# Moving the load, cast and DMA transposition of two batches' states to a later place in a fused attention and maxout kernel

## The chip, the cores and the metric

One core of one Trainium2 chip. The metric is device time in microseconds (us) of one execution. A profile covers the span from the first to the last instruction, some 1.8 us shorter than the time that is measured. Engines in the profile: PE is TensorE (PEld its weight loads), ACT is ScalarE, DVE is VectorE, POOL is GpSimd, SP is SyncE, which here only issues DMAs. L200 is line 200 of the kernel file.

## The reference

`x` is (8, 8, 512, 64): batch, head, token, width. `state` is (8, 8, 32, 64). Attention goes both ways between tokens and states; the result, 4352 rows of 512, goes through a maxout layer of three weights W and an output weight. The kernel folds the states into W (tile `G`), which changes nothing here.

```python
scores = x @ state.T / 8;    a  = softmax(scores);   xread = a @ state
scores2 = state @ x.T / 8;   a2 = softmax(scores2);  sread = a2 @ x
x = concatenate([xread, sread], axis=2)          # -> (8*544, 512)
h = maximum(maximum(x @ w1, x @ w2), x @ w3)
out = h @ w_out                                  # float32
```

## The kernel before

The order of instructions on each engine is set by hand and is the order of the calls below. States are kept for two batches at a time in a block-diagonal tile `bds[k]`; `bds[1]` serves batches 2 and 3. It is made in four steps: load in float32, cast (each state twice side by side), transposition, and placing (two copies into the diagonal blocks).

```python
def load_st(k, eng):
    eng.dma_start(out=st_f[k], in_=state[2 * k:2 * k + 2]...)          # 128 KB, float32
def states_cast(k, cast):
    cast(out=st[k], in_=st_f[k].unsqueeze(2).to_broadcast((128, 4, 2, D)))
def states_transpose(k, dma):
    if dma:
        nc.sync.dma_start_transpose(out=stT[k], in_=st[k]...)
    else:                                                              # TensorE, used for k = 0
        for t in range(4):
            nc.tensor.transpose(stT[k][:, t, :], st[k][:, t]..., ident)
def states_place(k, copy):
    for c in range(2):
        copy(out=bds[k][r, :, :, c, :]..., in_=stT[k][r]...)
def states(k, copy):
    states_transpose(k, False); states_place(k, copy)
def x_pad(b): nc.gpsimd.tensor_copy(...)     # x of a batch into columns with ones between
```

The schedule around it, with cuts (`pool` is a copy on GpSimd, `act` on ScalarE, `dve` on VectorE):

```python
    x_transpose(1, 0, act)
    load_st(1, nc.scalar)
    ...
    softmax(1, 1, 2, (nc.gpsimd.tensor_mul, J))
    load_w(3, (2,))                          # the last part of W
    states_cast(1, pool)
    states_transpose(1, True)
    load_x(2)
    nc.gpsimd.dma_start(out=wout_sb, in_=moe_w_out...)
    for k in range(2, B // 2):
        load_st(k, nc.gpsimd)
    load_x(3)
    load_x(4)
    ...                                      # GpSimd clears x_pads and bds[1..3]
    states_place(1, pool)
    x_maxout(0, 1)
    ...
    x_maxout(1, 2)
    for k in range(2, B // 2):
        states_cast(k, pool)
    x_pad(2)
    x_maxout(0, 4)
    x_transpose(2, 0, dve)
    x_maxout(0, 5)
    g_cols(1, (4, 5), defer=(False, True))
    x_transpose(2, 1, act)
    x_maxout(1, 3)
    scores(2, 0, 2)                          # first reader of bds[1]
    softmax(2, 0, 2, (nc.gpsimd.tensor_mul, J))
    x_transpose_dma(3)
    states_transpose(2, True)
```

The softmax here doesn't subtract the row's maximum and nothing guards it: scores larger than these inputs give would overflow.

## Time and profile before

| | before |
|---|---|
| time, median of 4 runs (lowest to highest) | 154.53 us (154.02 to 155.31) |
| span of the profiled run | 152.9 us |
| TensorE busy | 145.8 us, 95% |
| `bds[1]` complete | 31.0 us |
| scores of batch 2 start on TensorE | 33.55 us |
| from there to the end | 119.3 us |

A timeline line reads: start, length, engine, line of the kernel, operation, output from input, shapes, how many; in brackets how long the engine stood idle before it and what ended that. In the chain of work that ended last, the name after the two times is what the whole program waited for at that moment. The lines of before are in the prediction. The chain view puts the start of an instruction where its predecessor's modelled end is, so it has 33.72 us for the scores where the timeline has 33.55; from here on starts are the timeline's.

### The profile page before, as it was taken

The page shows a single profiled execution, that of the slowest core. Times are in us where ns is not written, and L with a number is a line of the kernel's source. Part 1 is how long each engine was busy: PE and PEld are TensorE (multiplying, and loading weights), DVE is VectorE, ACT ScalarE, POOL GpSimd, SP SyncE. Part 2 cuts the span into 40 slices and gives each one's busy share as a digit, 9 for nine tenths or more (in the row PEclk, how much of TensorE's full clock was granted, in tenths as well). Part 3 has the DMA queues.
Part 4 walks back from the last instruction along what each step waited for, and adds up shares of the span by engine and source line. Part 5 has one row for each costly group of instructions (what it writes and reads, how often), then busy time and mean ns, then how long its engine had stood idle before and what let it go on. Part 6 is the DMA issues. An engine that isn't in the chain of part 4 may idle for free.

```text
span 152.9 us, 3490 instructions
## 1 busy us (share of the span) xinstructions
PE 145.8 (95%) x1382; PEld 70.7 (46%) x1382; DVE 97.8 (64%) x177; ACT 94.0 (62%) x145; POOL 66.4 (43%) x80
## 2 busy tenths in 40 slices
PE   6987899999999999999999999999999999999990
PEld 2544443554453445344534453445344556665450
DVE  3488768768827685768576767776767684566010
ACT  3655788686848656865686568656865637332440
POOL 8988599737421882088308310821082100100410
PEclk9999999999999999999999999999999999999999
DMA  3999999999939999989485973061206120210473
GB/s 119 189 181 203 194 166 85 202 237 197 268 63 178 143 187 281 177 115 199 172 178 81 190 166 138 7 198 46 107 14 196 47 103 0 83 57 0 162 254 137
DMA packets 37520, 21.85 MB, mean 143 GB/s; under 512 B 22528, under 2 KB 35072, under 8 KB 37504
## 3 DMA queue, kind: packets, MB, share of 16 engines
q0 software_dynamic: 17184, 14.94, 54.3%
q1 hardware_dynamic: 20032, 6.43, 22.8%
q10 hardware_dynamic: 288, 0.26, 0.6%
q8 instruction: 11, 0.18, 0.5%
q14 instruction: 5, 0.04, 0.1%
HBM read 15.20 MB, written 8.91 MB: 158 GB/s over the span
## 4 chain that ended last, share of the span: by engine, by line
PE 83%; POOL 5%; DMA 5%; ACT 2%; issue 1%; DVE 1%; POOLq 0%; DVEq 0%
PE pw L377 43%; PE po L416 28%; DMA w<-in_moe_w_dram 5%; PE pg L301 4%; POOL w L109 2%; PE ps L200 2%; POOL x L80 2%; PE pg L327 1%; PE psr L267 1%; ACT G L333 1%; PE ph L408 1%; ACT t L382 1%; POOL a L220 1%; DVE t L385 0%; DVE den L213 0%
## 5 line engine op out<-in xcount | busy, mean ns | idle before, releaser
L377 PE MATMUL pw<-aT,G 128*128 128x512 bf16 x288 | 69.2, 379 | 0.4 <-ACT G L333 0.4
L385 DVE TENSOR_TENSOR t<-t,pw 128x512 bf16<-128x512 bf16 (+1 forms) x54 | 35.0, 649 | 29.0 <-ACT t L382 28.5
L416 PE MATMUL po<-wout,ht 128*128 128x512 bf16 x198 | 47.2, 379 | 0.2 <-DVE t L385 0.2
L377 PEld LDWEIGHTS <-G 128*128 128x128 bf16 x288 | 26.7, 98 | 32.1 <-issue 2.9
L386 DVE TENSOR_TENSOR ht<-t,pw 128x512 bf16<-128x512 bf16 (+1 forms) x54 | 35.5, 657 | 5.6
L382 ACT CAST t<-pw 128x512 bf16<-128x512 f32 (+1 forms) x54 | 30.5, 565 | 12.0 <-PE pw L377 11.2
L419 ACT COPY osb<-po 128x512 f32<-128x512 f32 x33 | 19.3, 586 | 28.5 <-PE po L416 28.5
L416 PEld LDWEIGHTS <-ht 128*128 128x128 bf16 x198 | 18.8, 98 | 24.1 <-issue 2.8
L430 POOL DMA_DIRECT2D out_dram<-osb x14 | 7.9, 566 | 47.8 <-ACT osb L419 42.0
L220 POOL TENSOR_TENSOR a<-e,rden 128x1024 bf16<-128x1024 bf16 (+2 forms) x10 | 15.3, 1532 | 25.8 <-DVE rden L215 16.2
L308 ACT CAST G<-pg 128x1024 bf16<-128x1024 f32 x24 | 24.5, 1021 | 2.3 <-PE pg L301 1.6
L246 POOL COPY xp<-x 128x2048 bf16<-128x2048 bf16 x6 | 11.3, 1884 | 0.0
L213 DVE TENSOR_REDUCE den<-e 128x32 f32<-128x1024 bf16 (+1 forms) x10 | 10.0, 996 | 1.7 <-ACT e L205 1.6
L333 ACT CAST G<-pg 128x768 bf16<-128x768 f32 x11 | 8.8, 808 | 2.2 <-PE pg L327 2.2
L109 POOL DMA_DIRECT2D w<-in_moe_w_dram x12 | 9.2, 782 | 0.6 <-DMA x<-in_x_dram 0.6
L377 PE MATMUL pw<-ats,w 128*128 128x256 bf16 x72 | 8.7, 272 | 0.0
L205 ACT ACTIVATE e<-ps 128x1024 bf16<-128x1024 f32 x6 | 6.2, 1029 | 3.7 <-PE ps L200 3.7
L377 PEld LDWEIGHTS <-w 128*128 128x128 bf16 x72 | 7.0, 98 | 1.9
L301 PE MATMUL pg<-w,bd 64*32 64x512 bf16 x192 | 7.5, 381 | 0.0
L127 PE MATMUL idle<-zero 128*128 128x512 bf16 x16 | 6.1, 528 | 1.2 <-DVE zero L85 1.2
L153 POOL COPY bd<-stT 64x512 bf16<-64x512 bf16 x6 | 6.5, 1077 | 1.1 <-DMA stT<-st 0.9
L200 PEld LDWEIGHTS <-xT 128*128 128x128 bf16 x128 | 5.0, 98 | 2.1 <-DVE t L385 0.3
(61 smaller groups left out, 85.9 us busy)
## 6 DMA issues: line engine op xcount, KB each, us to landing
out_dram<-osb POOLq DMA_DIRECT2D x14, 512.0 KB, 3.6
x<-in_x_dram POOLq DMA_DIRECT2D x6, 512.0 KB, 9.2
w<-in_moe_w_dram POOLq DMA_DIRECT2D x6, 256.0 KB, 6.6
x<-in_x_dram POOLq DMA_DIRECT2D x3, 256.0 KB, 6.5
w<-in_moe_w_dram POOLq DMA_DIRECT2D x6, 128.0 KB, 6.7
wout<-in_moe_w_out_dram POOLq DMA_DIRECT2D x1, 768.0 KB, 11.6
out_dram<-osb SPq DMA_DIRECT2D x3, 256.0 KB, 2.0
x0f<-in_x_dram SPq DMA_DIRECT2D x1, 512.0 KB
```

Source lines behind the costliest of these rows:

```text
L109: nc.gpsimd.dma_start(out=w_slices(w_sb, c)[:, :, i, :], in_=w[:, :, m0 * 128:m1 * 128])
L220: mul(out=a[b][:, r, g0:g1].rearrange("p j g s n -> p j (g s) n"), in0=e[b][:, r, g0:g1].rearrange("p j g s n -> p j (g s) n"), in1=rden[: ...
L246: nc.gpsimd.tensor_copy(out=x_pads[b % 2][:, 2:2 + 2 * H * PW].rearrange("p (k c) -> p k c", c=PW)[:, :, 0:2 * D], in_=x_sb[b][:, 0:XW].re ...
L301: nc.tensor.matmul(ps[g][32 * s:32 * s + 32], bd(b, 2 * s + g)[64 * g:64 * g + 64, g, :], w_sb[64 * g:64 * g + 64, s, c0:c1], start=True, ...
L308: copy(out=G[b][:, :, c0:c1], in_=p[:, :, 0:n])
L333: copy(out=m_cols(G[b], m), in_=pv)
L377: nc.tensor.matmul(pw[i][:, 0:n], lhs(i, k), rhs(k), start=(k == 0), stop=(k == nk - 1))
L382: nc.scalar.copy(out=t0[:, 0:n], in_=pw[0][:, 0:n])
L385: nc.vector.tensor_max(t1[:, 0:n], t0[:, 0:n], pw[1][:, 0:n])
L386: nc.vector.tensor_max(ht[b][:, m, :], t1[:, 0:n], pw[2][:, 0:n])
L416: nc.tensor.matmul(p, ht[b][:, m, j * 128:(j + 1) * 128], wout_sb[:, m, :], start=(m == 0), stop=(m == NM - 1))
L419: act(out=o[:, j, :], in_=p)
```

## The change

The intent: the states of batches 2 and 3 are not needed before 33 us, so their load need not share the DMA engines with W, which is needed at 15 us. It is moved behind all of W; cast and transposition follow once it is in, and GpSimd fills the time of the transposition with the padding of x of batch 2.

```diff
     x_transpose(1, 0, act)
-    load_st(1, nc.scalar)
     sread(0)
...
     load_w(3, (2,))
-    states_cast(1, pool)
-    states_transpose(1, True)
+    load_st(1, nc.gpsimd)
     load_x(2)
...
     for k in range(1, B // 2):
         nc.gpsimd.memset(bds[k], 0.0)
-    states_place(1, pool)
+    states_cast(1, pool)
+    states_transpose(1, True)
     x_maxout(0, 1)
...
     x_maxout(1, 2)
+    x_pad(2)
+    states_place(1, pool)
     for k in range(2, B // 2):
         states_cast(k, pool)
-    x_pad(2)
     x_maxout(0, 4)
```

## The prediction

> **What bounds the kernel now.** I read the page first. The rows of busy shares put TensorE (PE) at 95% of a span of 152.9 us, and the row of slices (each digit a tenth of busy time, 3.8 us a slice) has nines from the seventh slice on. So from about 25 us to the end TensorE is the bound, and a gap put into that stretch is paid in full. The DMA row is at nine over the first eleven slices, up to some 40 us.
>
> ```profile
> PE 145.8 (95%) x1382; PEld 70.7 (46%) x1382; DVE 97.8 (64%) x177; ACT 94.0 (62%) x145; POOL 66.4 (43%) x80
> PE   6987899999999999999999999999999999999990
> DMA  3999999999939999989485973061206120210473
> ```
>
> Next the chain that ended last (start in us, length in us, what). It is TensorE from about 15 us on; before that it is a load of W, and then a short stretch over ScalarE, VectorE and GpSimd.
>
> ```profile
> 7.70 7.33 DMA w<-in_moe_w_dram
> ...
> 15.06 0.40 PE pg L327 x8
> ...
> 18.02 1.05 POOL a L220
> ...
> 32.42 1.29 PE pw L377 x6
> 33.72 0.47 PE ps L200 x16
> 34.18 1.29 PE po L416 x6
> ```
>
> The line to look at is L200 at 33.72: the scores of batch 2. They are the first readers of the block-diagonal states of batches 2 and 3 (tile bd, index 1), the only tile whose making the change moves. They follow the maxout before them without a gap. Third, the timeline of GpSimd (POOL), which makes that tile:
>
> ```profile
> 19.01 0.80 POOL L109 DMA_DIRECT2D w<-in_moe_w_dram  x1
> 19.82 0.62 POOL L136 CAST st<-stf 128x512 bf16<-128x512 f32 x1
> 20.37 0.89 POOL L70 DMA_DIRECT2D x<-in_x_dram  x1
> ...
> 25.05 2.82 POOL L479 MEMSET bd<- 128x1024 bf16 x3
> 28.80 2.20 POOL L153 COPY bd<-stT 64x512 bf16<-64x512 bf16 x2 [0.94 <-DMA stT<-st]
> 33.34 1.17 POOL L136 CAST st<-stf 128x512 bf16<-128x512 f32 x2 [2.33 <-DMA stf<-in_state_dram]
> 34.46 1.89 POOL L246 COPY xp<-x 128x2048 bf16<-128x2048 bf16 x1
> 37.38 1.91 POOL L220 TENSOR_TENSOR a<-e,rden 128x1024 bf16<-128x1024 bf16 x1 [1.04 <-DVE rden L215]
> ```
>
> The cast of the states is at 19.82, the transposition is issued right behind it, and it runs while GpSimd issues loads and clears tiles: of its whole latency GpSimd waits for only 0.94 us. The tile is complete at 31.0, which is 2.7 us before TensorE wants it. That 2.7 us is all the slack there is. Last, the DMA issues, asked for in small windows so that each line is one transfer (the last number is us from issue to landing): the states of batches 2 and 3 as loaded now, then their transposition at 20.46, then the same transposition of the next states at 39.81.
>
> ```profile
> stf<-in_state_dram ACTq DMA_DIRECT2D x1, 128.0 KB, 5.5
> stT<-st SPq DMA_TRANSPOSE x1, 8.2
> stT<-st SPq DMA_TRANSPOSE x1, 3.8
> ```
>
> The same shape took 8.2 us when the load of x of batch 2 and of w_out were in flight, and 3.8 us when the loads were over. This spread is the main uncertainty.
>
> **What the Trainium skill says.** (1) "DMA: Bandwidth & Descriptors", section "Queues, rings and completion order": each DMA engine goes round-robin between the queues that have work, packet by packet, so a transfer from one queue is slowed by traffic of the others. The trace agrees: 8.2 us against 3.8. (2) The same page, "Rules for kernel authors": to overlap a DMA with compute, issue it early and wait late. The kernel before does it (0.94 us waited of 8.2); the change does the reverse. (3) "TensorE: Matmul & The Clock Gate", "The HAM clock gate": TensorE falls to half its clock after an idle window of some 3.4 us. Here the only long idle stretch is the end: the last matmul ends at 149.2, and the windows view (busy us and count per engine, then granted clock, DMA share, GB/s) shows half clock 3.4 us later:
>
> ```profile
> 152.60:152.85 0.25, 0.00 (x0) 0.00 (x0) 0.00 (x0) 0.00 (x0) 0.00 (x0) 0.50 0.00 0
> ```
>
> So a stall of over about 3.4 us in mid-kernel may cost more than itself.
>
> **The change, part by part.** Work is neither added nor removed; instructions move. The order of instructions on each engine confirms it: TensorE and VectorE keep theirs, ScalarE loses one DMA issue, GpSimd gains one.
>
> *The load of the states, 128 KB, from ScalarE's queue at 9.6 us to GpSimd's queue behind the last part of W.* It lands at about 15.1 now, beside the part of W that the chain waits for until 15.02; TensorE stands 0.65 us for it. With that load away I choose that this part lands 0.3 us earlier (an estimate: 128 KB at the 203 GB/s of that stretch is 0.65 us, and about half of it lies ahead of that part's last bytes). Everything up to the scores of batch 2, GpSimd's stream too, moves up by 0.3 us. ScalarE's issue costs nothing; GpSimd pays about 0.57 us (two such issues take 1.14 in its timeline).
>
> *GpSimd's stream.* At 19.82 the cast of 0.62 goes and the issue of 0.57 comes, so the clearing of the tiles still ends at 25.05 + 2.82 = 27.87, or 27.6 with the 0.3. The load issued at 19.8 is behind only the last part of W (issued 19.01, landing 5.7 us later, at 24.7), so it has landed by about 26 and the cast doesn't wait. Cast 27.6 to 28.2; transposition issued at 28.2.
>
> *The transposition.* Its landing L is what decides. The padding of x of batch 2 (1.89 us) fills 28.2 to 30.1 of it; the rest GpSimd waits. At 28.2 the queue still holds the end of w_out, the other states and x of batches 3 and 4 (the last lands at 39.3 now), so it is the loaded case, not the quiet one. With the early transposition gone, those loads get ahead somewhat. I choose L = 6.8, between 5 and 8.5.
>
> *The placing.* 0.1 us after the landing two copies start, 2.20 us: the tile is complete at 28.2 + 6.8 + 0.1 + 2.2 = 37.3.
>
> *TensorE.* It would be ready for the scores at 33.7 - 0.3 = 33.4, and stands until 37.3: a stall of 3.9 us. Against now, the scores start 37.3 - 33.7 = 3.6 us later; in general L - 3.2. Behind them TensorE is back to back, so nearly all stays. Give-back: one idle of 0.17 us at 41.1 may go, -0.2. Clock: a stall of 3.9 us is a little over one idle window, so a quarter chance of a drop that costs about half of a window each time, some 2 us: +0.4 in the mean. The padding moved ahead of the placing, and the two later casts (1.17 us) behind it, cost nothing: the softmax product comes 3.7 us after the start of the scores anyway (37.38 against 33.72). Sum: 3.6 - 0.2 + 0.4 = +3.8, so 154.66 + 3.8 = 158.5 us.
>
> **The rivals.** *The transposition is quick.* With the early one gone the loads before it are done sooner, and the DMA queue thins. At L = 3.8 the scores start only 0.6 us late, and the time is about 155.2. For it: the second transposition took that. Against it: 1 MB of x is still to come at 28.2, and its last landing is at 39.3. *W lands much earlier and pays for it.* The chain's 0.65 us stand at 15.06 is the most that can be won there, so this can't outweigh the rest; and as GpSimd's stream is in the same chain, both move together. Were there no wait at the scores, the time would be 154.3. *The stall trips the clock.* With L = 8.2 the stall is over 5 us, half clock follows for some us, and the time is 154.66 + 5.0 + 2 = 161.7. *Another wait takes the place:* x of batch 2 lands at about 29.1 now, just ahead of its transposes at 29.3; one more load ahead of it could delay it, but the early transposition that shared the engines with it is gone, which should advance it instead. If it came later, that wait would be swallowed by the stall at the scores.
>
> **Range and chances.** L from 5 to 8.5 gives +1.8 to +5.3; with the give-back and the clock's part, 156.4 to 160.8, centre 158.5. The line of 2% is +3.1 us, that is L of about 6.2 with the other terms at their means; I put L above it a little more often than not. Faster by 2% would need 3 us out of a stretch where TensorE is idle for about that much in all: 0.01. Within 2%: 0.37. Slower: 0.62.
>
> **What would show it.** In the changed kernel's profile: the cast of these states on GpSimd at about 27.6, right behind the clearing, with no wait; a new wait of GpSimd's placing for the transposition, about 5 us instead of 0.94; a new wait of TensorE at L200 for the placing, 3 to 5 us, and scores at about 37 instead of 33.7; the chain going through GpSimd's clearing, the cast, the transposition and the placing; the wait for W at 15.06 shorter by a few tenths; the stretch from the scores to the end unchanged in length, or longer where the granted clock shows 0.50. The prediction is wrong if the transposition lands in 4 us or less, if the states' load lands late and the cast waits, or if the clock drops for a long time.

## The result, and the profile after

The changed kernel takes 161.06 us (median of 4 runs, 159.75 to 161.89), the kernel before 154.53. The ratio is 1.041, with a 95% interval from 1.032 to 1.05. A ratio here is the mean time of one kernel's fast runs over the mean of the other's fast runs of the same rounds, so it is not quite the ratio of the two medians. Executions over 1.5% slower than the fastest of the same kernel are left out of the means. The change is slower, and the time is 0.26 us above the range that was predicted.

From the page of the changed kernel, the rows that answer to those of before (1366 matmuls instead of 1382, because some records are missing from this trace):

```profile
PE 146.9 (92%) x1366; PEld 71.3 (45%) x1382; DVE 98.2 (61%) x177; ACT 94.2 (59%) x145; POOL 67.1 (42%) x81
PE   7988899942999999999999999999999999999991
PEclk9999999995599999999999999999999999999999
DMA  4999999999919597876959596034304230030274
```

There is a hole in TensorE's row in the ninth and tenth slices, from about 33 us, and in the row of the granted clock two slices at half speed. GpSimd's timeline:

```profile
27.68 0.68 POOL L136 CAST st<-stf 128x512 bf16<-128x512 f32 x1
29.45 1.89 POOL L246 COPY xp<-x 128x2048 bf16<-128x2048 bf16 x1 [1.09 <-DMA x<-in_x_dram]
36.58 2.13 POOL L153 COPY bd<-stT 64x512 bf16<-64x512 bf16 x2 [5.23 <-DMA stT<-st]
```

The cast runs where it was expected, at 27.68 without a wait. The padding waits 1.09 us for x of batch 2, which costs nothing, as the placing behind it would only wait longer. The placing waits 5.23 us for the transposition; before it waited 0.94. The chain that ended last now goes through it (start, length, what):

```profile
27.81 0.56 POOL st L136
28.37 0.02 issue
28.39 8.07 DMA stT<-st
...
36.58 1.05 POOL bd L153
37.62 0.05 issue
37.67 1.05 POOL bd L153
38.72 0.04 issue
38.76 1.01 PE ps L200 x16
```

So the scores of batch 2 start at 38.76 instead of 33.55, 5.2 us later. The windows view (stretch, its length, busy us and count of PE, PEld, DVE, ACT, POOL, then granted clock, DMA share, GB/s) shows what came of TensorE's idle time:

```profile
33.70:36.40 2.70, 0.00 (x0) 0.00 (x0) 1.38 (x2) 0.92 (x2) 0.00 (x0) 1.00 1.44 165
36.50:38.70 2.20, 0.00 (x0) 0.00 (x0) 0.00 (x0) 0.00 (x0) 2.07 (x2) 0.50 1.20 161
38.80:43.20 4.40, 4.18 (x24) 2.14 (x25) 1.57 (x2) 1.61 (x2) 1.66 (x3) 0.50 1.13 161
43.30:46.00 2.70, 2.70 (x58) 1.25 (x63) 1.49 (x3) 1.01 (x2) 1.29 (x1) 1.00 0.22 29
```

TensorE is idle from 33.7 us. At 36.5 its clock is halved, and it stays halved until 43.3, so TensorE works for 4.5 us (38.8 to 43.3) at half speed. From the scores to the end it now takes 159.83 - 38.76 = 121.1 us instead of 119.3. The two together are the whole: 5.2 us of a later start and 1.8 us of a longer rest make the 7.0 us by which this profiled span is longer (159.83 against 152.86).

### The profile page after: what moved, and what is told of

Its sections match the earlier page's. It is cut to its first block, busy times and chain, and to the rows that moved or that the text cites.

```text
span 159.8 us, 3472 instructions
## 1 busy us (share of the span) xinstructions
PE 146.9 (92%) x1366; PEld 71.3 (45%) x1382; DVE 98.2 (61%) x177; ACT 94.2 (59%) x145; POOL 67.1 (42%) x81
## 4 chain that ended last, share of the span: by engine, by line
PE 72%; POOL 12%; DMA 10%; issue 2%; ACT 1%; DVE 1%; POOLq 0%; DVEq 0%
PE pw L377 36%; PE po L416 27%; DMA stT<-st 5%; DMA w<-in_moe_w_dram 5%; PE pg L301 4%; POOL w L109 3%; PE ps L200 2%; POOL x L70 2%; POOL bd L477 2%; POOL x L80 2%; PE psr L267 1%; POOL bd L153 1%; POOL stf L58 1%; PE ph L408 1%; POOL a L220 1%
## 5 line engine op out<-in xcount | busy, mean ns | idle before, releaser
L200 PE MATMUL ps<-bd,xT 128*128 128x64 bf16 x96 | 4.2, 201 | 5.1 <-POOL bd L153 5.1
```

What stands on the lines that cost most here:

```text
L200: nc.tensor.matmul(p[:, 2 * jj:2 * jj + 2, g - g0, s, :], xT[b][:, h, jj, :], bd(b, h).rearrange("p c n -> p (c n)"), start=(g == g0 and s ...
```

## The experiments

They had to settle three things: whether the clock really accounts for the longer rest, why the transposition takes 8 us here, and whether the new place of the load has a part in it. Twelve runs, two of them repeats, were made, with the kernel before run beside them; all gave right results.

### The clock: TensorE kept busy in the stall

```diff
+    keep_busy(16)          # 16 idle matmuls of 512 columns
     scores(2, 0, 2)
```

> The changed kernel with 16 idle matmuls of 512 columns (about 3.5 us) put on TensorE ahead of the scores of batch 2, into the stall. Theory (stall of 5.1 us, and half clock from 36.5 to 43.3 us that it brings about): the clock stays at 1.00, the stretch from the scores to the end goes back from 121.0 us to the 119.2 us of the kernel before, and the time falls by some 2 us, from 161 to about 159. Rival (the 1.9 us come from another wait behind the scores, or the clock falls for another reason): the time stays at 161.

Median 157.88 us, ratio to before 1.0215 (1.0165 to 1.0265). The clock is 1.00, and from the scores to the end it takes 156.17 - 37.29 = 118.9 us, not 121.1. The theory holds for the rest. The time fell by 3 us rather than 2, though, against a changed kernel that had run on another chip; so both were run again side by side.

> The changed kernel as it is, for a direct comparison on the same chip with the run that keeps TensorE busy. Theory: 160 to 162, half clock for 3.4 or 6.8 us in each run, the faster runs being those with the shorter half clock.

> The changed kernel with the 16 idle matmuls in the stall, again, beside the changed kernel on the same chip. Theory (the lost clock is worth half of the matmul time that runs at half speed): faster than the changed kernel by 1.8 to 2.3 us, clock at 1.00. Rival (the idle matmuls also shorten the stall in some way, as the first comparison over two chips, 157.9 against 160.9, could be read): faster by 3 us or more.

The changed kernel took 160.56 us (median), ratio 1.0396 (1.0352 to 1.044); with the idle matmuls 157.86, ratio 1.0215 (1.0169 to 1.0262; three of its four runs counted, the fourth, 160.16 us at clock 1.000, was classed as slow, and no run explains it). The means of the fast runs are 160.61 and 157.82, 2.8 us apart: between what theory and rival expected. One more expectation was missed: the faster runs of the changed kernel were not those with the shorter half clock. The slowest of the four, 161.09 us, has the highest mean clock (0.989), the fastest, 160.22, one of the lowest (0.978). TensorE's timeline of the warm kernel:

```profile
32.31 3.62 PE L127 MATMUL idle<-zero 128*128 128x512 bf16 x16
37.06 0.63 PE L200 MATMUL ps<-bd,xT 128*128 128x64 bf16 x16 [1.13 <-POOL bd L153]
```

From the scores to the end this takes 155.94 - 37.06 = 118.9 us. The profiled run of the changed kernel beside it has half clock for one window only, from 38.38 to 41.79, and takes 159.23 - 39.04 = 120.2. The clock is 1.3 us of that pair; the other 2 us are a scores' start at 37.06 instead of 39.04, of which 0.9 is a shorter transposition (7.5 against 8.4 us) and 1.1 lies before 15 us, where the two kernels are the same. In both warm profiles the first part ran about 1 us ahead of that of the two changed ones. Why, stays open: over all profiles the first matmul that waits for the second part of W starts anywhere from 13.8 to 15.7 us (17.0 with the dummy below).

The profiles give a dose and an answer. The clock's changes are read from the trace's clock records:

| profile | TensorE idle before the scores | scores start | half clock | of it behind that start | scores to end |
|---|---|---|---|---|---|
| warm, first and second | 1.2 and 1.1 us | 37.29 and 37.06 | none | 0 | 118.9 and 118.9 |
| cast ahead (below) | 3.8 | 36.95 | 36.17 to 39.59 | 2.6 | 120.1 |
| changed, second | 5.5 | 39.04 | 38.38 to 41.79 | 2.8 | 120.2 |
| changed | 5.1 | 38.76 | 36.46 to 43.28 | 4.5 | 121.1 |
| old load (below) | 3.7 | 37.01 | 35.39 to 42.22 | 5.2 | 121.8 |

Each us at half speed behind the scores' start costs about half a us. Two single runs below, whose loads differ, fit too: "x later" (stall of 3.3 us, 3.3 us of half clock behind the start, 120.5 to the end) and "dummy first" (2.8, 2.8 and 120.6). The kernel before, which has neither stall nor half clock, takes 119.3 there; the warm ones are 0.4 shorter, so that much of a stall is given back. Whether that is because the other engines caught up meanwhile was not looked at.

### The transposition: the first of a program, or a loaded queue?

In both kernels the slow transposition was the first one of the program. So one of the same shape, of no use, was put ahead of it:

```diff
+    nc.sync.dma_start_transpose(out=dummy, in_=e[0][:, 0:2]...)
     load_w(2, (1, 2))
```

> The changed kernel with a transposition of the same shape, of no use, issued at about 9 us. Theory A (the 8.1 us come from the loads in flight): the states' transposition still takes 7 to 8.5 us, the dummy 5 us or more. Theory B (the first DMA transposition of a program is the slow one, whatever is in flight): the dummy takes about 8 us and the states' one about 4, so the scores start at about 35 us and the time is about 156.

The states' transposition, now the second, was issued at 30.64 and took 7.55 us; the dummy took 8.5 us. Theory B falls. (The dummy also held W up: TensorE waited 3.1 us for it and lost clock from 16.0 to 22.8 us, and the run took 162.97 us.) Then the loads were taken out of the way:

```diff
     load_st(1, nc.gpsimd)
     load_x(2)
-    (w_out, states of batches 4 to 7, x of batches 3 and 4)
...
     states_place(1, pool)
+    (w_out, states of batches 4 to 7, x of batches 3 and 4)
```

> The changed kernel with the loads of w_out, of the other states and of x of batches 3 and 4 moved behind the placing, so that only x of batch 2 is ahead of the transposition. The whole will be slower, as TensorE then waits for w_out; what is read is the transposition. Theory A (loads in flight): 3.5 to 4.5 us from issue to landing, and its packets begin within 2 us of the issue instead of 4. Theory B (first transposition is slow): 8 us as in the changed kernel.

As the DMA issues have it (last number: us from issue to landing):

```profile
stT<-st SPq DMA_TRANSPOSE x1, 3.9
```

3.9 us instead of 8.1, with the same shape, engine and place in the program. The whole took 163.29 us, since TensorE then waited for w_out. With less taken away:

```diff
     load_st(1, nc.gpsimd)
     load_x(2)
     ... (w_out and the states stay)
-    load_x(3)
-    load_x(4)
...
     states_place(1, pool)
+    load_x(3)
+    load_x(4)
```

> The changed kernel with only the loads of x of batches 3 and 4 moved behind the placing; w_out and the other states stay ahead of the transposition. Theory A' (its packets first wait for what is queued on each engine at its issue, then share with what follows): first packet still about 4 us after the issue, but the tail is shorter as x isn't there to share with: 5.5 to 6.5 us in all. Rival (x behind it is what holds it up): first packet within 2 us, 4 us in all.

It took 8.0 us: a miss for both. As two issues fewer stood ahead of the cast, the transposition was also issued 2.6 us earlier, with more of w_out in front of it; so this run shows that the end of x of batch 2, w_out and the states alone can hold it up for 8 us, and leaves open what x of the later batches adds. The DMA view of the changed kernel, cut to the stretch from the issue at 28.39 to just before its first packet, and to the rest, tells where the time goes (queue, packets, MB, share of the 16 engines' time, over 100% where packets overlap):

```profile
q0 software_dynamic: 844, 0.87, 124.0%
...
stT<-st SPq DMA_TRANSPOSE x1, 8.1
```

```profile
q0 software_dynamic: 1084, 0.60, 110.0%
q1 hardware_dynamic: 544, 0.13, 37.0%
```

From 28.4 to 32.2 us the engines move only GpSimd's queue (q0). The transposition's 512 packets of 256 bytes (q1, with some small ones) come after that, beside x of the later batches. Counted in the same way from the packets of each trace (queued: what GpSimd had issued before the transposition's issue, less what had begun to move by then):

| profile | issued at | KB queued on q0 at the issue | first packet after | packets of q0 per engine until then | landed after |
|---|---|---|---|---|---|
| quiet | 24.45 | 174 | 1.3 us | 14 | 3.9 us |
| before | 20.46 | 302 | 1.9 | 32 | 8.2 |
| load first (below) | 19.89 | 344 | 1.9 | 38 | 7.5 |
| x later | 25.75 | 989 | 3.7 | 40 | 8.0 |
| changed | 28.39 | 1832 | 4.0 | 55 | 8.1 |
| dummy first | 30.64 | 1696 | 4.0 | 58 | 7.6 |
| old load (below) | 27.45 | 1682 | 4.0 | 58 | 7.2 |
| cast ahead (below) | 25.16 | 2312 | 4.1 | 62 | 9.5 |

The packets of the fifth column alone would prove little, since a longer wait lets more packets through. What was queued at the issue sets the short waits apart from the long ones; from 989 to 2312 KB the wait hardly grows, and why it ends at some 4 us is not shown.

So the 8.2 us before and the 8.1 after are made of different parts, and their likeness says nothing of the traffic. Before, the queue was short, the packets began after 1.9 us, half had begun at 2.6, and then single packets of both queues stood for up to 1.7 us, the last came at 6.1, and the landing another 2.1 us later. After, the wait for the first packet is half of the whole (4.0 us), the packets take 3.5 and the landing 0.6 more.

### An earlier cast and transposition, load left where it is

```diff
     load_x(4)
+    states_cast(1, pool)
+    states_transpose(1, True)
     ...                              # clearing of x_pads and bds
-    states_cast(1, pool)
-    states_transpose(1, True)
```

> The changed kernel with cast and transposition of the states moved up, right behind the issues of the loads and ahead of the clearing of the tiles (load still behind W, padding and placing where the change has them). Theory (only the issue time of the transposition and its loaded latency of 7 to 8.2 us count): issue at about 25 us instead of 28, tile complete at about 34.5 to 35.5, stall at the scores 1 to 2.5 us, short enough that the clock stays at 1.00; about 155.8 to 157.3. Rival (the latency ends when the loads end, whenever the transposition is issued): landing at 35 to 36.5 as in the changed kernel, time 159 or more.

Median 158.19 us, ratio 1.0206 (1.0149 to 1.0264; three of the four runs counted, the profiled one was classed as slow). Half a miss: one run, 156.26 us at a mean clock of 0.996, lies where the theory put it; the two other fast ones, 158.09 and 158.28 at 0.988 and 0.985, lost clock as the profiled one did.

```profile
25.16 1.38 SPq L144 DMA_TRANSPOSE stT<-st  x1
...
34.76 2.14 POOL L153 COPY bd<-stT 64x512 bf16<-64x512 bf16 x2 [4.42 <-DMA stT<-st]
```

It was issued 3.2 us earlier and landed 1.8 us earlier (34.64 against 36.46), 0.5 of which is the first part of the program running ahead (14.54 against 15.02 at the wait for W). The rest of the head start was eaten by a longer way, 9.5 us: it waited behind the same loads. Issuing into a full queue buys little; the kernel before issues at 20.46, before that queue is filled.

### The place of the load

```diff
     x_transpose(1, 0, act)
+    load_st(1, nc.scalar)
     ...
-    load_st(1, nc.gpsimd)
     load_x(2)
```

> The changed kernel with the load of the states back on ScalarE's queue at its old place; only the later cast, transposition and placing remain of the change. Theory (the place of the load has no part in the time: its packets ran at 13 to 15 us, when the part of W that the chain waits for was nearly in): within 1 us of the changed kernel, about 160 to 161.5, stall of 4.5 to 5.5 us at the scores. Rival (W lands earlier without it, by 0.3 us or more, as the prediction has it): slower than the changed kernel by as much, with a wait for W that is longer by 0.3 us or more.

Median 159.76 us, ratio 1.0329 (1.0253 to 1.0405), which overlaps the changed kernel's 1.041 and 1.0396. The stall was 3.7 us, less than expected, with a transposition of 7.2 us, and its four runs had half clock for 7.3, 3.5, 0 and 5.1 us (worked out from each run's mean clock and span, the end of the run included), with times of 160.65, 158.88, 158.68 and 160.64. That spread hides a few tenths, and the place of the load needed a comparison without a stall. So the states were transposed by TensorE instead, as those of batches 0 and 1 are, with the load in either place:

```diff
     load_x(4)
+    states_cast(1, pool)
     ...
-    states_cast(1, pool)
-    states_transpose(1, True)
     ...
-    states_place(1, pool)
     ...
     x_maxout(0, 5)
+    states(1, act)                   # 4 transposes on TensorE, 2 copies on ScalarE
     g_cols(1, (4, 5), defer=(False, True))
```

> The load behind W as in the change, but the states are transposed by TensorE (4 transposes, placed by ScalarE with two copies, in the middle of the second maxout before they are needed), the cast ahead of the clearing; no DMA transposition of them. Theory (the DMA transposition under load is the whole cause, and the load behind W frees W's last needed part by some 0.5 us): no wait at the scores, clock 1.00, no wait for W at 15 us; 153.8 to 155.0, that is 0.99 to 1.003 of the kernel before. Rival (the load behind W costs by itself, by delaying x of batch 2): a wait for x of batch 2 at its transposes, 155.5 or more.

> As the run before it in this call, but with the states' load on ScalarE's queue at its old place. Theory (the load in W's way costs some 0.5 us at the wait for W): 0.3 to 0.6 us slower than the run with the load behind W, with a wait of TensorE for W at 14.5 to 15.1 us. Rival (no effect of the load's place): the same within 0.2 us.

With the load behind W: 154.72 us, ratio 1.0004 (0.9986 to 1.0023). With the load at its old place: 154.83 us, ratio 1.0029 (1.0013 to 1.0044). The means of 21 and 22 fast runs are 154.57 and 154.87, so the load's new place is worth 0.3 us (95% interval, worked out from the spread of the two sets of runs: 0.05 to 0.55), against 0.3 to 0.6 expected. The expected absence of a wait for W was not seen: the profiled run with the load behind W waits 1.1 us for it at 14.91, the other 0.65 us at 14.82. The first had been faster up to there, so a single profile does not show where the 0.3 us come from. In both, the clock stays up and no DMA wait is left at the scores, though another is:

```profile
34.36 0.52 PE L200 MATMUL ps<-bd,xT 128*128 128x64 bf16 x12 [0.60 <-ACT xT L182]
```

ScalarE's two copies delay its copy of the transposed x. The load was also tried in the one stretch where the DMA engines are not yet full, with everything else as in the kernel before:

```diff
     nc.sync.dma_start(out=x0_f, in_=x_heads(0, 0)[1])
+    load_st(1, nc.sync)
...
-    load_st(1, nc.scalar)
```

> The kernel before with the states' load issued on SyncE's queue in the first two us, when the DMA engines are not full, and all the rest as it was. Theory (the load beside W costs some 0.5 us): 154.0 to 154.6, no wait for W at 15 us. Rival (it takes the same from the first loads of x): the same as the kernel before or slower by up to 0.5 us, with the wait moved to the first transposes.

Median 154.39 us, ratio 0.9994 (0.9975 to 1.0013): the same within the interval, which both theory and rival allowed. The wait for W at 15 us is gone from its profile; the weight loads of TensorE wait 0.9 us for the cast of the first x instead of 0.4, as the rival had it.

### A version that beats both

ScalarE stands idle for 1.2 us one maxout earlier, so TensorE's transposes and ScalarE's copies go there:

```diff
     x_maxout(0, 4)
+    states(1, act)
     x_transpose(2, 0, dve)
     x_maxout(0, 5)
-    states(1, act)
```

> The version with the load behind W and the states transposed by TensorE, with these transposes one maxout earlier, where ScalarE stands idle for about 1.2 us. Theory (in the first form ScalarE's two copies delay the transposed x of batch 2, and TensorE waits 0.6 us for it): no wait at the scores, 153.9 to 154.4, that is 0.3 to 0.6 us faster than the first form. Rival: TensorE now waits elsewhere for ScalarE, same as the kernel before within 0.2 us.

Median 153.84 us of 22 runs, ratio to before 0.9965 (0.9946 to 0.9985). It is inside 2%, but its interval lies below 1; it is the fastest version here (the profiled run, 155.09 us, is one of its two slowest). It differs from the kernel before in two things, the load's place and the transposition on TensorE; as the place alone was worth about 0.3 us above, this run does not show what the transposition on TensorE gives by itself. TensorE's timeline has the transposes (L148) and the scores without a wait:

```profile
29.93 0.39 PE L148 MATMUL pt<-ident,st 128*128 128x128 bf16 x4
30.16 0.61 PE L178 MATMUL spare<-ident,x 128*128 128x128 bf16 x8
...
34.24 0.63 PE L200 MATMUL ps<-bd,xT 128*128 128x64 bf16 x16
```

## Why the prediction was right or wrong

The direction and the mechanism were right; the size was wrong by 2.6 us (158.5 against 161.06), just outside the range. Step by step:

- **TensorE is the bound, and a gap there is paid in full.** Right: 5.2 us of later start and 1.8 us of longer rest are all of the 7.0 us between the two profiled spans.
- **GpSimd's stream.** Right: cast at 27.68 for a predicted 27.6, no wait, transposition at 28.39 for 28.2.
- **The load away from W, 0.3 us.** As an effect it was measured at 0.3 us between the two versions with TensorE's transposes. In the profile of the changed kernel TensorE's wait for W is shorter, as foretold (0.17 us instead of 0.65), but no time was won: TensorE came to it later, and the first matmul on the second part of W starts at 15.02 against 15.06.
- **The transposition, L = 6.8.** Too low: 8.07, and 7.2 to 9.5 in every loaded run here. The argument for shading it below the 8.2 us of before ("those loads get ahead somewhat") was the wrong one. They did not get ahead: w_out landed at 33.20 (32.85 before), the last x at 39.98 (39.24). And with the cast behind the loads' issue the transposition met a longer queue (1832 KB instead of 302), and its first packet waited 4.0 us instead of 1.9. L + the missing 0.3 gave a scores' start 5.2 us later instead of 3.6. The prediction's own formula, L - 3.2, gives 4.9 with the L that was measured.
- **The clock, "a quarter chance" of some 2 us, +0.4 in the mean.** This is the step that failed. All eight runs of the changed kernel have a mean clock of 0.977 to 0.989, so half clock in each. The size of one drop was right: half speed behind the scores' start cost 1.3 us (against the warm kernel) where one window was lost and 2.2 where two were. It was the chance that was wrong. The stall was 5.1 us, not 3.9; but the quarter chance also took it that a whole window of 3.4 us has to be idle. In the changed kernel TensorE worked for about 0.6 us of the 3.4 before the drop, with the old load for 1.3, and the profiled stalls of 2.8 (dummy first), 3.3 (x later), 3.7 (old load) and 3.8 us (cast ahead) all lost clock. So a stall of 3.9 us would probably have lost it too. It was not certain: one run of four with the old load (mean clock 1.000) and one with the cast ahead (0.996) show no such loss.
- **Give-back 0.2.** It was 0.4 (119.3 against 118.9 in both warm profiles).
- **The rivals.** "The stall trips the clock", told as 161.7 for L = 8.2, is what happened, at 161.06. The quick transposition is what the quiet run shows (3.9 us), but needs the loads gone. x of batch 2 did land later (29.40 against 29.04): GpSimd's padding, which now stands earlier, waited 1.09 us for it, TensorE's transposes of it still began at 29.44 without a gap (29.33 before), and the delay was swallowed as foretold. What was given a side place should have been the centre.

In the sum, the terms were 3.6 - 0.2 + 0.4 = 3.8. Measured on the profiled spans they are 5.2 - 0.4 + 2.2 = 7.0, with the give-back and the clock's part read against the warm kernels. So the longer transposition (1.6 us more at the scores' start) and the clock (1.8 us more) share the miss almost evenly, but only the clock's term lay far from what was allowed for: L was within its range of 5 to 8.5. One reading of a line was loose, without effect: the first slice of the DMA row is 3, not 9.

## What to carry to other kernels

A DMA is "hidden" only by its slack, so compare its latency under the traffic that it will meet, not the latency it had elsewhere; here a transposition on SyncE's queue, moved behind the issue of large loads on GpSimd's, waited 4 us for its first packet. When TensorE is the bound and is made to stand for some three us, count its clock's loss as part of the price from the start (every profiled stall of 2.8 to 5.5 us without idle matmuls had it), and try idle work in the gap to tell the two apart. A small transposition that is due in the middle of the loading can go to TensorE, even if TensorE is the bound: with four transposes there the later load and cast cost nothing (ratio 1.0004, and 0.9965 in the better place), while the DMA of 8 us made it 1.041.

## What the Trainium skill lacked or had wrong

- "TensorE: Matmul & The Clock Gate", "The HAM clock gate": it has the clock fall after an idle window of some 3.4 us. The length agrees: every change in these traces lies on a grid of 3.413 us from the first (before: 43 steps; changed: 9, then 2, then 34). But a window need not be idle. Laid on this grid, the windows at full clock of all 14 traces divide by TensorE's busy time: each of the 22 with at most 1.3 us of work was followed by half clock (old load 1.3), none with 1.5 us or more was (dummy first, near its end, 1.5). The clock came back after windows with 2.6 us of work or more (cast ahead 2.6), not after those with up to 2.4 (dummy first, 2.4). These are readings of modelled busy times, not exact limits; that page gives no amount of work.
- "DMA: Bandwidth & Descriptors", "Queues, rings and completion order": round-robin by packets is right as far as it goes (the two queues do share once the transposition's packets have begun), but it doesn't foretell the wait before the first packet, 3.7 to 4.1 us with 989 to 2312 KB queued on the other queue, 1.3 us with 174.
- The same page, "Specifications": first-byte latency on the path of SyncE and ScalarE is given as about 0.6 us. For this transposition, from the start of the issue to the first packet, it was 1.3 us at the least (the issue itself takes 1.3) and 4.1 at the most.
- No page gives a cause for single packets of both queues of one core standing for up to 1.7 us while a transposition and loads run together (before, at 22.9 to 24.6 us; 1.8 us in "load first"); no run here explains it.
